# A weight decoder's rates per step changed, four steps without decoding, and two VectorE chains staggered

## The chip, the core and the metric

The kernel runs as one program on one core of a Trainium2 chip. The time is device microseconds (us) of that core for one execution; where several executions were timed, their median is given. Engines are named as in the profile: PE is TensorE (PEld its weight loads), DVE is VectorE, ACT is ScalarE, POOL is GpSimd, SP issues the DMAs.

## The reference: clustered attention and two MLPs

The inputs q, k, v are (2, 8, 768, 64) in single precision; the five weight matrices of the MLPs are in double precision, and the kernel reads each number as two 32-bit words. In short:

```
mask   = argmax(q_n @ c_n) == argmax(k_n @ c_n)      # cluster of each query and key
attn   = softmax(where(mask, q @ k^T / 8, -1e9))
x      = (attn @ v), heads side by side               # 1536 tokens x 512
x      = (sigmoid(x @ w_gate) * (x @ w_val)) @ w_out  # first MLP,  512 -> 1536 -> 512
out    = (relu(x @ w_in)^2) @ w_out2                  # second MLP, 512 -> 2048 -> 512
```

## The kernel before: steps, two instruction streams beside each other, and their order

**Precision.** Every matmul operand is a pair of fp32r tiles, a high part (rounded copy) and a low part (what is left). A product takes three matmuls of 128 columns of weights by 512 tokens: high by high, high by low, low by high (L339 to L341, and L416).

**Steps.** After the attention, which ends near 300 us, the two MLPs are a list of steps. The tokens are in three groups g = 0, 1, 2 of 512. The hidden layer is cut into slices j of 128, and four slices make a chunk (CH = 4). Per chunk there are 12 steps of the first layer (named "g" in the first MLP, gate and value of slice j for group g, 24 matmuls; named "i" in the second, 12 matmuls), and then 12 steps "o" of the output layer, in the order g outer, j inner, 12 matmuls each. An "o" step adds slice j into four PSUM banks, d = 0 to 3, one for each 128 of the 512 outputs. With the last j of a chunk the four sums are complete: DVE adds each into an SBUF tile `part` (L422; in the first chunk ACT copies it, L420). In the last chunk of the first MLP `part` is the second MLP's x: ACT makes its high part (`x_hi`, L427), DVE the low part (`x_lo`, L428), d after d. Below, o8 to o11 are the output weights of that chunk, i0 to i3 the first weights of the second MLP. The first steps of the second MLP run in the order (i0,g0), (i1,g0), (i0,g1), (i1,g1), (i0,g2), (i1,g2), and then i2 and i3.

**Decoding.** A weight slice comes from HBM as 512 KB of 64-bit numbers (`wraw`, two buffers) and is made into high and low parts by three stages, each a few instructions (`SLOTS`): stage 1 is `wmag` on ACT (L210) and L235, L239 on DVE; stage 2 is `wtop` (L242), `wmag` (L246) on DVE and the high part on ACT (L224); stage 3 is L215, L227, L230 on DVE, which ends with the low part. Stage 3's first instruction is followed by the fetch of the next raw slice into the buffer that it has read, on SP's queue.

**What sets the order.** The order is written out while the program is built. Each engine runs its own instructions in that order, and waits on the others by semaphores. Ahead of each step `decode(n)` adds `RATE` of the step's layer to a credit (at most 3.0) and places one decoding stage for each whole credit, provided that a buffer is free. Whatever is still missing for step n + 1 is placed at once. Then the step itself is placed, with its evictions. `presplit` makes the high and low parts of an "o" step's activations (`shi` on ACT, L382; `slo` on DVE, L383) four steps ahead; it has five buffers, so `shi` waits until PE has finished the "o" step that used its buffer, five "o" steps before. PSUM has four banks `bank_a` and four `bank_b`; "o" steps take `bank_b` for g = 0 and 2, `bank_a` for g = 1, the other steps `bank_a`. An "i" step's bank is emptied by ACT's relu (L375, written to `sg`) and its square (L376).

```
RATE = {"g": 2.25, "i": 1.25, "o": 1.25}
```

Of the kernel before, what the change touches and what calls it, by code (L numbers as in the profile page):

```python
# [14 lines left out]
ALU = mybir.AluOpType  # L15
# [56 lines left out]
def cluster_attention_two_mlps(  # L72
# [13 lines left out]
    nc = tc.nc  # L86
    B, H, S, D = q.shape
    NCL = centroids.shape[1]
    P = 128
# [3 lines left out]
    F1 = w_gate.shape[1]  # L93
# [6 lines left out]
    NG = B * S // TG  # L100

    def f32(ap):
        return ap.bitcast(F32)
# [5 lines left out]
    def x_tiles():  # L109
        return [[xp.tile([P, KD, TG], F32R, name=f"x_{t}{g}") for t in ("hi", "lo")] for g in range(NG)]  # L110
# [7 lines left out]
    CH = 4  # L118
    NA, NW, NWO = CH + 2, 4, CH + 2
    steps = []  # L120
# [17 lines left out]

    AHEAD = 4

    RATE = {"g": 2.25, "i": 1.25, "o": 1.25}
    pools = {}

    def open_weights():
# [122 lines left out]
    flight, credit = [], [0.0]  # L267
# [7 lines left out]
    def slot(n):  # L275

        moved = False
        for state in list(flight):
            d, parts, at = state
            if at == 1 and not buffer_free(d, n):  # L280
                break
            for x in SLOTS[at]:
                parts[x]()
            state[2] += 1
            moved = True
            if state[2] == len(SLOTS):
                flight.remove(state)
        if not moved and not flight and decoded[0] < len(weights):
            d = decoded[0]
            if buffer_free(d, n + 2):  # L290
                flight.append([d, decode_next(), 0])
                for x in SLOTS[0]:
                    flight[-1][1][x]()
                flight[-1][2] = 1
                moved = True
        return moved

    def decode(n):
        credit[0] = min(credit[0] + RATE[steps[n][1]], 3.0)
        while credit[0] >= 1.0 and slot(n):  # L300
            credit[0] -= 1.0

        while any(first_use[key] <= min(n + 1, len(steps) - 1) and key not in W for key in weights[: decoded[0] + 1]):
            need = [k for k in weights if first_use[k] <= n + 1 and k not in W]
            if not slot(n):
                assert all(first_use[k] > n for k in need), (n, need)
                break

    with tc.manual_schedule():
# [22 lines left out]
        def bank(side):  # L332
            return pools[side].tile([P, TG], F32, name=f"bank_{side}")
# [10 lines left out]
        act, parts, banks, split, sgs = {}, {}, {}, {}, {}  # L344
# [41 lines left out]
        def outer(step):  # L386
            mlp, _, j, g = step
            if step[0] == 2 and g == NG - 1 and j >= F2 // P - CH:

                if j == F2 // P - 1:  # L390
                    for d in range(KD):
                        for jj in range(F2 // P - CH, F2 // P):
                            outer_part((mlp, "o", jj, g), (d,))
                return
            outer_part(step, range(KD))

        def outer_part(step, ds_):
            mlp, _, j, g = step
            hi, lo = split[step]
            chunk = j // CH  # L400
            first, last = j % CH == 0, j % CH == CH - 1
            final = j == (F1 if mlp == 1 else F2) // P - 1
            w = W["o", mlp, j]
            for d in ds_:
                ds = slice(d * P, (d + 1) * P)
                if first:
                    banks[g, d] = bank("ba"[g % 2])
                bk = banks[g, d]

                pairs = (  # L410
                    [(w[:, 0, ds], hi), (w[:, 0, ds], lo), (w[:, 1, ds], hi)]
                    if mlp == 1
                    else [(hi[:, ds], w[:, 0]), (hi[:, ds], w[:, 1]), (lo[:, ds], w[:, 0])]
                )
                for n, (st, mv) in enumerate(pairs):
                    nc.tensor.matmul(bk, st, mv, start=(first and n == 0), stop=(last and n == 2))  # L416
                if last:
                    if chunk == 0:
                        parts[g, d] = pools["part"].tile([P, TG], F32, name=f"part{g}_{d}")
                        nc.scalar.copy(parts[g, d], bk)  # L420
                    else:
                        nc.vector.tensor_tensor(out=parts[g, d], in0=bk, in1=parts[g, d], op=ALU.add)  # L422
                    if final and mlp == 1:
                        if 2 not in xin:
                            xin[2] = x_tiles()
                        h, l = (t[:, d] for t in xin[2][g])
                        nc.scalar.copy(h, parts[g, d])  # L427
                        nc.vector.tensor_tensor(out=l, in0=parts[g, d], in1=f32(h), op=ALU.subtract)  # L428
                    elif final:
                        b, c = divmod(g * KD + d, NB)  # L430
                        nc.sync.dma_start(
                            out=out[b * S : (b + 1) * S].rearrange("(p c) d -> c p d", c=NB)[c], in_=parts[g, d]
                        )


        with ExitStack() as ac:
# [418 lines left out]
            for n in range(N + LAG + 4):  # L855
# [27 lines left out]
                if u is not None:  # L883
                    e = pp.tile([P, S], F32, name="p")
                    nc.scalar.activation(  # L885
                        out=e.rearrange("p (m n) -> p m n", m=2),
# [47 lines left out]
        with ExitStack() as mc:  # L934
            pools["o"] = mc.enter_context(tc.tile_pool(name="wop", bufs=NWO, reuse_waits="tile"))
            pools["part"] = mc.enter_context(tc.tile_pool(name="part", bufs=1, reuse_waits="tile"))
            pools["split"] = mc.enter_context(tc.tile_pool(name="split", bufs=AHEAD + 1, reuse_waits="tile"))
            pools["b"] = mc.enter_context(tc.tile_pool(name="ps_b", bufs=4, space=PSUM, reuse_waits="tile"))

            run = {"g": gated, "i": relu2, "o": outer}  # L940
            for n, step in enumerate(steps):
                if n < 2:
                    continue
                if n + AHEAD < len(steps) and steps[n + AHEAD][1] == "o":
                    presplit(steps[n + AHEAD])
                decode(n)
                run[step[1]](step)
# [29 lines left out]
```

## Time and profile before

| what | value |
|---|---|
| median of three runs | 862.56 us (861.41 to 864.62) |
| the profiled execution | 861.74 us, of which its span is 860.0 us |
| PE busy | 814.5 us, 95% of the span |
| DVE, ACT, POOL busy | 621.5, 448.7, 215.1 us |
| granted clock of PE, mean | 0.981 of full speed |
| slice 28 of 40 (580.5 to 602.0 us) | PE busy 5 tenths; every slice beside it 9 |
| a weight's DMA, issue to landing | 3.3 us (output weights), 3.6 to 3.8 us (the others) |

The page gives busy time by engine, then 40 slices of the span, then the chain of work that ended last, then groups of instructions. A row of a timeline has the start and the duration in us, engine, line, operation, output <- inputs, and in brackets how long the engine was idle before it and who released it. PE's matmuls are pipelined, so that the distance between two starts, not the duration, is what one costs. The same holds on DVE, where a following instruction starts before the recorded end of the one before.

### The profile page before, as it was taken

The page shows a single profiled execution, that of the slowest core. Times are in us where ns is not written, and L with a number is a line of the kernel's source. Part 1 is how long each engine was busy: PE and PEld are TensorE (multiplying, and loading weights), DVE is VectorE, ACT ScalarE, POOL GpSimd, SP SyncE. Part 2 cuts the span into 40 slices and gives each one's busy share as a digit, 9 for nine tenths or more (in the row PEclk, how much of TensorE's full clock was granted, in tenths as well). Part 3 has the DMA queues.
Part 4 walks back from the last instruction along what each step waited for, and adds up shares of the span by engine and source line. Part 5 has one row for each costly group of instructions (what it writes and reads, how often), then busy time and mean ns, then how long its engine had stood idle before and what let it go on. Part 6 is the DMA issues. An engine that isn't in the chain of part 4 may idle for free.

```text
span 860.0 us, 11716 instructions
## 1 busy us (share of the span) xinstructions
PE 814.5 (95%) x4069; PEld 694.7 (81%) x4069; DVE 621.5 (72%) x1129; ACT 448.7 (52%) x900; POOL 215.1 (25%) x339
## 2 busy tenths in 40 slices
PE   7697998998999999999999999995999999999998
PEld 5587888998999888788888888784888888888886
DVE  5596997898998557864678647887879589588033
ACT  7586797898888223441233123333755652552530
POOL 1467798898898200000000000000000000000000
PEclk9898999999999999999999999998999999999999
DMA  9764845855631212230222112211223123120012
GB/s 203 176 135 120 180 110 129 184 115 131 148 103 40 68 50 74 74 98 24 74 74 73 50 50 74 64 59 50 77 71 122 50 74 98 50 74 24 1 50 98
DMA packets 68107, 75.67 MB, mean 88 GB/s; under 512 B 29680, under 2 KB 56304, under 8 KB 68048
## 3 DMA queue, kind: packets, MB, share of 16 engines
q1 hardware_dynamic: 68048, 74.93, 32.7%
q8 instruction: 32, 0.52, 0.3%
q14 instruction: 27, 0.22, 0.1%
HBM read 45.12 MB, written 3.15 MB: 56 GB/s over the span
## 4 chain that ended last, share of the span: by engine, by line
PE 77%; DVE 9%; ACT 4%; DMA 3%; POOL 3%; issue 2%; SPq 1%; POOLq 0%; ACTq 0%; DVEq 0%
PE bank_b L416 15%; PE bank_a L340 12%; PE bank_a L339 12%; PE bank_a L341 12%; PE bank_a L416 8%; PE t L765 6%; PE s L747 6%; PE o L783 3%; PE o L784 3%; PE t L590 1%; DMA st_q<-lo_q 1%; DVE part L422 1%; DMA x<-oc 1%; DVE x_lo L428 1%; ACT x_hi L427 1%
## 5 line engine op out<-in xcount | busy, mean ns | idle before, releaser
L339 PE MATMUL bank_a<-x_hi,w 128*128 128x512 f32 x480 | 188.9, 394 | 8.8 <-ACT sg L375 8.8
L340 PE MATMUL bank_a<-x_lo,w 128*128 128x512 f32 x480 | 190.0, 396 | 0.5 <-POOL x_lo L813 0.5
L341 PE MATMUL bank_a<-x_hi,w 128*128 128x512 f32 x480 | 188.3, 392 | 0.0
L339 PEld LDWEIGHTS bank_a<-x_hi,w 128*128 128x128 f32 x480 | 90.6, 189 | 30.3 <-ACT sg L375 9.2
L773 DVE TENSOR_TENSOR pt_lo<-t,pt_hi 128x384 fp32r<-128x384 f32 x192 | 97.5, 548 | 23.8 <-ACT pt_hi L767 23.0
L383 DVE TENSOR_TENSOR slo<-act,shi 128x512 fp32r<-128x512 f32 x84 | 57.6, 687 | 71.4 <-ACT shi L382 67.4
L340 PEld LDWEIGHTS bank_a<-x_lo,w 128*128 128x128 f32 x480 | 90.6, 189 | 20.8 <-POOL x_lo L813 1.0
L341 PEld LDWEIGHTS bank_a<-x_hi,w 128*128 128x128 f32 x480 | 90.5, 189 | 20.4
L818 POOL TENSOR_SCALAR p<-p,nm,ones 128x768 f32<-128x768 f32 x96 | 95.7, 997 | 20.1 <-DVE nm L817 12.8
L765 PE MATMUL t<-ident,p 128*128 128x128 f32 x576 | 83.8, 282 | 16.1 <-POOL lo_q L546 14.0
L864 DVE TENSOR_REDUCE nm<-s 128x1 f32<-128x768 f32 x96 | 91.0, 948 | 4.5 <-PE s L747 4.4
L885 ACT ACTIVATE p<-s,nm 128x768 f32<-128x768 f32 x96 | 88.4, 921 | 7.5 <-DVE nm L817 3.8
L767 ACT CAST pt_hi<-t 128x384 fp32r<-128x384 f32 x192 | 83.6, 488 | 16.0 <-DMA x_lo<-pt_hi 7.8
L765 PEld LDWEIGHTS t<-ident,p 128*128 128x128 f32 x576 | 69.4, 145 | 23.1 <-POOL lo_q L546 15.0
L747 PE MATMUL s<-st_k,st_q 128*128 128x384 f32 (+1 forms) x336 | 81.4, 365 | 2.2 <-ACT p L885 1.1
L365 DVE TENSOR_TENSOR act<-bank_a,sg 128x512 f32<-128x512 f32 x36 | 24.9, 692 | 76.9 <-PE bank_a L341 73.0
L416 PE MATMUL bank_b<-wo,shi 128*128 128x512 f32 x256 | 79.0, 390 | 0.0
L224 ACT CAST w<-wtop 128x512 fp32r<-128x512 f32 x38 | 23.6, 621 | 99.5 <-DVE wtop L242 99.5
L382 ACT CAST shi<-act 128x512 fp32r<-128x512 f32 x84 | 51.1, 615 | 32.1 <-PE bank_b L416 20.0
L783 PE MATMUL o<-pt_hi,vt 128*128 128x384 f32 x192 | 66.2, 345 | 0.4 <-ACT oc L789 0.4
L784 PE MATMUL o<-pt_lo,vt 128*128 128x384 f32 x192 | 65.4, 341 | 0.0
L416 PE MATMUL bank_b<-shi,wo 128*128 128x512 f32 x192 | 60.7, 392 | 1.5 <-DVE wo L230 1.5
(136 smaller groups left out, 1401.6 us busy)
## 6 DMA issues: line engine op xcount, KB each, us to landing
wraw<-in_moe_w_out_dram SPq DMA_DIRECT2D x28, 512.0 KB, 3.3
wraw<-in_moe_w_in_dram SPq DMA_DIRECT2D x16, 512.0 KB, 3.8
x<-oc SPq DMA_DIRECT2D x64, 96.0 KB, 2.9
wraw<-in_moe_w_gate_dram SPq DMA_DIRECT2D x11, 512.0 KB, 3.6
wraw<-in_moe_w_val_dram SPq DMA_DIRECT2D x11, 512.0 KB, 3.7
st_k<-hi_k SPq DMA_DIRECT2D x26, 192.0 KB, 4.1
st_q<-hi_q SPq DMA_DIRECT2D x26, 192.0 KB, 4.0
nat_v<-in_v_dram SPq DMA_DIRECT2D x8, 384.0 KB, 3.2
```

What stands on the lines that cost most here:

```text
L339: nc.tensor.matmul(bk, w[:, 0, ks], mov_hi[:, kk], start=(kk == 0), stop=False)
L340: nc.tensor.matmul(bk, w[:, 0, ks], mov_lo[:, kk], start=False, stop=False)
L341: nc.tensor.matmul(bk, w[:, 1, ks], mov_hi[:, kk], start=False, stop=(kk == KD - 1))
L416: nc.tensor.matmul(bk, st, mv, start=(first and n == 0), stop=(last and n == 2))
L747: nc.tensor.matmul(st[:, m, :NH], Q[i, e][: DEPTH[a], a, c * P : (c + 1) * P], K[i, e][: DEPTH[a], a, m * NH : (m + 1) * NH], start=(a == ...
L765: nc.tensor.transpose(tp[:, m, :], Pt[u][:, c * P : (c + 1) * P], ident)
L773: nc.vector.tensor_tensor(out=lo, in0=tp, in1=f32(hi), op=ALU.subtract)
L783: nc.tensor.matmul(o, vt, hi[:, c, :], start=(c == 0), stop=False)
L784: nc.tensor.matmul(o, vt, lo[:, c, :], start=False, stop=(c == NB - 1))
L818: nc.gpsimd.tensor_scalar(out=p, in0=p, scalar1=nm[:, 3:4], scalar2=ones, op0=ALU.mult, op1=ALU.mult)
L864: nc.vector.tensor_reduce(out=nms[n][:, 0:1], in_=st[n][:, :, :NH], axis=AX.XY, op=ALU.max, negate=True)
L885: nc.scalar.activation(out=e.rearrange("p (m n) -> p m n", m=2), in_=st.pop(n)[:, :, :NH], func=AF.Exp, bias=nms[n][:, 0:1], accum_out=nms ...
```

## The change: what it does

Three edits. The decoding rates per step become 2.8, 1.4 and 0.85 for "g", "i" and "o". In the last four steps of the first MLP (j = 8 to 11 of group 2) the rate is 0, so no stage of a decode is placed there. And where x's low parts are made, `x_lo` of sum d is placed behind `part` of sum d + 1, and the last one behind all.

```
--- before.py
+++ after.py
@@ -138,7 +138,7 @@
 
     AHEAD = 4
 
-    RATE = {"g": 2.25, "i": 1.25, "o": 1.25}
+    RATE = {"g": 2.8, "i": 1.4, "o": 0.85}
     pools = {}
 
     def open_weights():
@@ -296,7 +296,10 @@
         return moved
 
     def decode(n):
-        credit[0] = min(credit[0] + RATE[steps[n][1]], 3.0)
+        mlp, layer, j, g = steps[n]
+
+        rate = 0.0 if (mlp, layer) == (1, "o") and j >= F1 // P - CH and g == NG - 1 else RATE[layer]
+        credit[0] = min(credit[0] + rate, 3.0)
         while credit[0] >= 1.0 and slot(n):
             credit[0] -= 1.0
 
@@ -401,6 +404,7 @@
             first, last = j % CH == 0, j % CH == CH - 1
             final = j == (F1 if mlp == 1 else F2) // P - 1
             w = W["o", mlp, j]
+            lows = []
             for d in ds_:
                 ds = slice(d * P, (d + 1) * P)
                 if first:
@@ -420,17 +424,24 @@
                         nc.scalar.copy(parts[g, d], bk)
                     else:
                         nc.vector.tensor_tensor(out=parts[g, d], in0=bk, in1=parts[g, d], op=ALU.add)
+                    if lows:
+                        low_part(*lows.pop(0))
                     if final and mlp == 1:
                         if 2 not in xin:
                             xin[2] = x_tiles()
                         h, l = (t[:, d] for t in xin[2][g])
                         nc.scalar.copy(h, parts[g, d])
-                        nc.vector.tensor_tensor(out=l, in0=parts[g, d], in1=f32(h), op=ALU.subtract)
+                        lows.append((l, parts[g, d], f32(h)))
                     elif final:
                         b, c = divmod(g * KD + d, NB)
                         nc.sync.dma_start(
                             out=out[b * S : (b + 1) * S].rearrange("(p c) d -> c p d", c=NB)[c], in_=parts[g, d]
                         )
+            for low in lows:
+                low_part(*low)
+
+        def low_part(lo, whole, hi):
+            nc.vector.tensor_tensor(out=lo, in0=whole, in1=hi, op=ALU.subtract)
 
 
         with ExitStack() as ac:
```

**DVE, end of the first MLP.** In these rows `w_4137` and `w_4184` are the tiles of i2 and i3, `w1_68` that of i1, and `part2_d`, `x_lo2` belong to token group 2. Before:

```order
L215 SCALAR_TENSOR_TENSOR wbody_6334<-wraw_6264,wmag_6335 128x512
L227 TENSOR_TENSOR wtop_6336<-wtop_6336,w_4137 128x512
L230 TENSOR_TENSOR w_4137<-wtop_6336,wbody_6334 128x512
L235 TENSOR_SCALAR wbody_6400<-wraw_6314 128x512
L239 SCALAR_TENSOR_TENSOR wbody_6400<-wraw_6314,wbody_6400 128x512
L242 SCALAR_TENSOR_TENSOR wtop_6402<-wmag_6401,wbody_6400 128x512
L246 TENSOR_SCALAR wmag_6401<-wtop_6402 128x512
L215 SCALAR_TENSOR_TENSOR wbody_6400<-wraw_6314,wmag_6401 128x512
L227 TENSOR_TENSOR wtop_6402<-wtop_6402,w_4184 128x512
L230 TENSOR_TENSOR w_4184<-wtop_6402,wbody_6400 128x512
L422 TENSOR_TENSOR part2_0_4918<-bank_b_6367,part2_0_4918 128x512
L428 TENSOR_TENSOR x_lo2_6238<-part2_0_4918,x_hi2_6237 128x512
```

After:

```order
L444 TENSOR_TENSOR x_lo1_6236<-part1_3_4842,x_hi1_6235 128x512
L426 TENSOR_TENSOR part2_0_4904<-bank_b_6353,part2_0_4904 128x512
L426 TENSOR_TENSOR part2_1_4909<-bank_b_6357,part2_1_4909 128x512
L444 TENSOR_TENSOR x_lo2_6238<-part2_0_4904,x_hi2_6237 128x512
L426 TENSOR_TENSOR part2_2_4914<-bank_b_6361,part2_2_4914 128x512
L444 TENSOR_TENSOR x_lo2_6238<-part2_1_4909,x_hi2_6237 128x512
L426 TENSOR_TENSOR part2_3_4919<-bank_b_6365,part2_3_4919 128x512
L444 TENSOR_TENSOR x_lo2_6238<-part2_2_4914,x_hi2_6237 128x512
L444 TENSOR_TENSOR x_lo2_6238<-part2_3_4919,x_hi2_6237 128x512
L215 SCALAR_TENSOR_TENSOR wbody_6304<-wraw_6184,wmag_6305 128x512
L227 TENSOR_TENSOR wtop_6306<-wtop_6306,w1_68 128x512
L230 TENSOR_TENSOR w1_68<-wtop_6306,wbody_6304 128x512
```

The decodes of i2 and i3 stood ahead of group 2's sums, and now stand behind them; so does the last stage of i1, which stood ahead of group 1's sums before. `x_lo` of sum d is one place behind `part` of sum d + 1.

**ACT, the same place.** `x_hi1`, `x_hi2` are the high parts of groups 1 and 2, and `sg` the first relu of the second MLP, which empties the bank of (i0,g0). Before:

```order
L427 CAST x_hi1_6235<-part1_3_4850 128x512
L224 CAST w_4137<-wtop_6336 128x512
L210 ACTIVATE wmag_6401<-wraw_6314 128x512
L224 CAST w_4184<-wtop_6402 128x512
L427 CAST x_hi2_6237<-part2_0_4918 128x512
L427 CAST x_hi2_6237<-part2_1_4923 128x512
L427 CAST x_hi2_6237<-part2_2_4928 128x512
L427 CAST x_hi2_6237<-part2_3_4933 128x512
L210 ACTIVATE wmag_6451<-wraw_6384 128x512
L375 ACTIVATE sg_6470<-bank_a_6456 128x512
```

After:

```order
L433 CAST x_hi1_6235<-part1_3_4842 128x512
L433 CAST x_hi2_6237<-part2_0_4904 128x512
L433 CAST x_hi2_6237<-part2_1_4909 128x512
L433 CAST x_hi2_6237<-part2_2_4914 128x512
L433 CAST x_hi2_6237<-part2_3_4919 128x512
L210 ACTIVATE wmag_6423<-wraw_6264 128x512
L378 ACTIVATE sg_6442<-bank_a_6428 128x512
```

Two high parts of weights and a `wmag` have left the place between groups 1 and 2.

**DVE, first "o" steps of the first chunk.** `wo_4704` before and `wo_4688` after are the tile of the fourth output weight o3 (`wbody`, `wtop`, `wmag` with the numbers just below it belong to its decode); the `slo` are the presplits of the steps placed there. Before:

```order
L383 TENSOR_TENSOR slo_4678<-act_4216,shi_4677 128x512
L235 TENSOR_SCALAR wbody_4681<-wraw_4609 128x512
L239 SCALAR_TENSOR_TENSOR wbody_4681<-wraw_4609,wbody_4681 128x512
L383 TENSOR_TENSOR slo_4700<-act_4429,shi_4699 128x512
L242 SCALAR_TENSOR_TENSOR wtop_4683<-wmag_4682,wbody_4681 128x512
L246 TENSOR_SCALAR wmag_4682<-wtop_4683 128x512
L215 SCALAR_TENSOR_TENSOR wbody_4681<-wraw_4609,wmag_4682 128x512
L227 TENSOR_TENSOR wtop_4683<-wtop_4683,wo_4704 128x512
L230 TENSOR_TENSOR wo_4704<-wtop_4683,wbody_4681 128x512
```

After:

```order
L386 TENSOR_TENSOR slo_4658<-act_4165,shi_4657 128x512
L235 TENSOR_SCALAR wbody_4661<-wraw_4576 128x512
L239 SCALAR_TENSOR_TENSOR wbody_4661<-wraw_4576,wbody_4661 128x512
L386 TENSOR_TENSOR slo_4684<-act_4216,shi_4683 128x512
L242 SCALAR_TENSOR_TENSOR wtop_4663<-wmag_4662,wbody_4661 128x512
L246 TENSOR_SCALAR wmag_4662<-wtop_4663 128x512
L386 TENSOR_TENSOR slo_4704<-act_4434,shi_4703 128x512
L215 SCALAR_TENSOR_TENSOR wbody_4661<-wraw_4576,wmag_4662 128x512
L227 TENSOR_TENSOR wtop_4663<-wtop_4663,wo_4688 128x512
L230 TENSOR_TENSOR wo_4688<-wtop_4663,wbody_4661 128x512
```

Stage 2 of o3 stood behind the third `slo` of this stretch's presplits together with stage 3, and is now one step earlier, so that only stage 3 stands behind that `slo`. In the two later chunks of the first MLP the fourth output weight ends a step earlier in the same way.

## Rows read from the trace of the kernel before

**Rows 1.** Waits of TensorE (PE) from 300 us on: us in total, times, longest.

```profile
PE bank_a L339 <- ACT sg L375: 8.8, 1, 8.8
PE bank_b L416 <- DVE wo L230: 1.5, 3, 1.1
```

**Rows 2.** Timeline of PE, 583 to 614 us: start, duration, line, operands, idle before.

```profile
592.57 0.39 PE L341 MATMUL bank_a<-x_hi,w 128*128 128x512 f32 x1
601.74 0.80 PE L339 MATMUL bank_a<-x_hi,w 128*128 128x512 f32 x1 [8.78 <-ACT sg L375]
...
606.01 0.39 PE L340 MATMUL bank_a<-x_lo,w 128*128 128x512 f32 x1
```

**Rows 3.** Window: busy PE, PEld, DVE, ACT, POOL; granted clock; DMA share, GB/s.

```profile
596.00:598.00 2.00, 0.00 (x0) 0.00 (x0) 1.32 (x3) 0.62 (x1) 0.00 (x0) 0.50 0.00 0
```

**Rows 4.** Timeline of ScalarE (ACT), 575 to 614 us.

```profile
580.59 0.62 ACT L427 CAST x_hi<-part 128x512 fp32r<-128x512 f32 x1 [1.36 <-DVE part L422]
...
601.10 0.58 ACT L375 ACTIVATE sg<-bank_a 128x512 f32<-128x512 f32 x1
```

**Rows 5.** Timeline of VectorE (DVE), 575 to 612 us.

```profile
577.83 0.68 DVE L422 TENSOR_TENSOR part<-bank_a,part 128x512 f32<-128x512 f32 x1
...
579.87 0.68 DVE L422 TENSOR_TENSOR part<-bank_a,part 128x512 f32<-128x512 f32 x1
581.24 0.69 DVE L428 TENSOR_TENSOR x_lo<-part,x_hi 128x512 fp32r<-128x512 f32 x1 [0.69 <-ACT x_hi L427]
...
585.81 0.69 DVE L242 SCALAR_TENSOR_TENSOR wtop<-wmag,wbody 128x512 f32<-128x512 f32 x1
...
586.99 0.69 DVE L215 SCALAR_TENSOR_TENSOR wbody<-wraw,wmag 128x512 f32<-128x512 uint32 x1
587.60 0.69 DVE L227 TENSOR_TENSOR wtop<-wtop,w 128x512 f32<-128x512 f32 x1
588.32 0.69 DVE L230 TENSOR_TENSOR w<-wtop,wbody 128x512 fp32r<-128x512 f32 x1
...
593.31 0.68 DVE L422 TENSOR_TENSOR part<-bank_b,part 128x512 f32<-128x512 f32 x1
...
600.66 0.69 DVE L428 TENSOR_TENSOR x_lo<-part,x_hi 128x512 fp32r<-128x512 f32 x1 [0.68 <-ACT x_hi L427]
```

**Rows 6.** Timeline of PE, 578.5 to 583 us.

```profile
579.65 0.62 PE L416 MATMUL bank_b<-shi,wo 128*128 128x512 f32 x2
...
581.69 0.39 PE L416 MATMUL bank_b<-shi,wo 128*128 128x512 f32 x1
581.91 0.39 PE L339 MATMUL bank_a<-x_hi,w 128*128 128x512 f32 x1
```

**Rows 7.** Timeline of PE, 355.2 to 360.5 us.

```profile
356.57 0.86 PE L416 MATMUL bank_b<-shi,wo 128*128 128x512 f32 x2
...
358.80 0.73 PE L416 MATMUL bank_b<-shi,wo 128*128 128x512 f32 x2 [1.13 <-DVE wo L230]
...
360.30 0.39 PE L416 MATMUL bank_b<-shi,wo 128*128 128x512 f32 x1
```

**Rows 8.** Timeline of DVE, 346 to 361 us.

```profile
358.05 0.69 DVE L230 TENSOR_TENSOR wo<-wtop,wbody 128x512 fp32r<-128x512 f32 x1
```

**Rows 9.** Timeline of PE, 100 to 300 us: rows with an idle time.

```profile
108.51 0.92 PE L765 MATMUL t<-ident,p 128*128 128x128 f32 x6 [2.59 <-POOL lo_q L546]
...
140.35 0.92 PE L765 MATMUL t<-ident,p 128*128 128x128 f32 x6 [2.44 <-POOL lo_q L546]
...
173.16 0.92 PE L765 MATMUL t<-ident,p 128*128 128x128 f32 x6 [2.19 <-POOL lo_q L546]
```

**Rows 10.** Windows behind these three idle times, columns as in Rows 3.

```profile
108.50:116.00 7.50, 7.49 (x52) 7.28 (x52) 7.45 (x17) 7.31 (x19) 6.99 (x10) 1.00 0.11 27
...
140.40:146.00 5.60, 5.60 (x29) 5.42 (x30) 4.78 (x11) 4.66 (x12) 4.33 (x7) 0.70 0.11 27
...
173.20:178.00 4.80, 4.80 (x35) 4.63 (x35) 4.80 (x11) 4.80 (x13) 4.46 (x7) 1.00 0.10 23
```

More of the change, by code (lines that the diff above doesn't have):

```diff
@@ L139, in cluster_attention_two_mlps @@
     AHEAD = 4
-    RATE = {"g": 2.25, "i": 1.25, "o": 1.25}
+    RATE = {"g": 2.8, "i": 1.4, "o": 0.85}
     pools = {}
@@ L298, in decode @@
     def decode(n):
-        credit[0] = min(credit[0] + RATE[steps[n][1]], 3.0)
+        mlp, layer, j, g = steps[n]
+        rate = 0.0 if (mlp, layer) == (1, "o") and j >= F1 // P - CH and g == NG - 1 else RATE[layer]
+        credit[0] = min(credit[0] + rate, 3.0)
         while credit[0] >= 1.0 and slot(n):
@@ L403, in outer_part @@
             w = W["o", mlp, j]
+            lows = []
             for d in ds_:
@@ L422, in outer_part @@
                         nc.vector.tensor_tensor(out=parts[g, d], in0=bk, in1=parts[g, d], op=ALU.add)
+                    if lows:
+                        low_part(*lows.pop(0))
                     if final and mlp == 1:
@@ L427, in outer_part @@
                         nc.scalar.copy(h, parts[g, d])
-                        nc.vector.tensor_tensor(out=l, in0=parts[g, d], in1=f32(h), op=ALU.subtract)
+                        lows.append((l, parts[g, d], f32(h)))
                     elif final:
@@ L433, in outer_part, with low_part @@
                         )
+            for low in lows:
+                low_part(*low)
+        def low_part(lo, whole, hi):
+            nc.vector.tensor_tensor(out=lo, in0=whole, in1=hi, op=ALU.subtract)
         with ExitStack() as ac:
```

## The prediction

> **What bounds the kernel now.** I read the page's slices first (the table above has the one that matters): in nearly every slice of the MLPs TensorE is busy for nine tenths or more, and one stands out with five. So the MLPs take as long as TensorE's matmuls, plus what TensorE waits. The view of its waits from 300 us on names all of them [rows 1]: one of 8.8 us for an ACT relu, and three of together 1.5 us, the longest 1.1, for the low part of an output weight. A change to decoding and evictions can only give back these, and what hangs on them, or add new ones.
>
> The long wait lies at the passage to the second MLP. The last matmul before it starts at 592.57, the next at 601.74 [rows 2]. Undisturbed matmuls start 0.227 us apart, nine in 579.65 to 581.69 [rows 6]. So 9.17 - 0.23 = 8.94 us are lost there. While TensorE idles its granted clock falls to half, 0.50 in 596 to 598 [rows 3], and it is slow after the wait too: the ten distances from 601.74 to 606.01 take 4.27 us instead of 2.27, a loss of 2.0 [rows 2]. The passage costs 10.9 us.
>
> What ended the wait is read on the two engines behind it. ACT's relu at 601.10 [rows 4] empties the bank that (i0,g2) needs, and stands in ACT's order behind the four x_hi of group 2; each of those needs its `part`. VectorE begins group 2's sums only at 593.31 [rows 5], although TensorE finished them at 581.69 + 0.39 = 582.1 [rows 6]. Up to then VectorE was in a chain for group 1 (577.83 to 585.81) and two weight decodes (585.81 to 593.31) [rows 5]. The chain is slow: `part` at 579.87, x_hi on ACT at 580.59, x_lo at 581.24 [rows 4, 5]; with 0.61 for x_lo the next link starts 1.98 us later, and VectorE has idled 0.69 of it. Four links are 7.98 us (577.83 to 585.81).
>
> **The change part by part.**
>
> *Staggering.* Let the first `part` start at 0. x_hi starts 0.72 later and x_lo 1.37 later, as before, but the second `part` runs in between. From then on VectorE has something ready: at its pitch of 0.61 (586.99 to 587.60 [rows 5]) the order part, part, x_lo, part, x_lo, part, x_lo, x_lo gives the third x_lo at 3.81. The fourth `part` starts at 3.20, so its x_hi at 3.92 and its x_lo at 4.57; VectorE is free at 5.18. The chain costs 5.18 instead of 7.98.
>
> A rule of the Trainium skill speaks against this edit: the page VectorE: DVE Perf Modes, section The DRAIN you can't avoid, says that the next instruction does not start before the pipe has emptied, that semaphores between instructions cost nothing extra, and that only their number counts. By that, reordering the same eight instructions gives nothing, and the chain stays at 7.98. The rows differ: an instruction of 0.69 us is followed 0.61 later by the next [rows 5], and 0.69 of each link is marked as idle until ACT's x_hi, which is the time that the new order fills.
>
> *No decoding in the last four steps.* Between the chains of groups 0 and 1 VectorE had 16 instructions and has 11 (counted in the two orders), five less at some 0.6: 3.0 us. With 2.8 from group 0's stagger, group 1's chain starts near 577.83 - 5.8 = 572.0 and ends near 577.2. Nothing stands between it and group 2's any more, so group 2's chain starts when TensorE ends the first sum: 579.65 + 0.39 = 580.04 [rows 6]. Its x_lo is done near 585.2. TensorE wants it for (i0,g2), four steps of 12 x 0.227 = 2.72 after 581.91, at 592.8. The 8.94 us and the half clock go. What is late next is on ACT nothing: its relu of (i0,g0) now stands behind x_hi's end and one `wmag`, some 584 to 585, seven us before its bank is wanted.
>
> *The price: i1.* Its last stage now stands behind group 2's chain: L215 at 585.2, L227 0.61 later, L230 0.72 later (586.99, 587.60, 588.32 [rows 5]), at 586.55, done 0.69 later at 587.24. The first matmul to read this low part is the third of (i1,g0), 14 x 0.227 after 581.91: 585.08. TensorE waits 587.24 - 585.08 = 2.2 us. Behind that matmul everything else on TensorE waits with it. Bounds: if VectorE were held only by TensorE's last sum (582.08, then 1.37, 0.61, 0.61, 0.72, 0.69), 1.0; if the stagger gave nothing, 2.2 + 2.8 = 5.0. I take 2.2, from the rows' own pitches.
>
> Does a wait of 2.2 lower the clock? Three waits of that size stand in the attention: 2.59, 2.44 and 2.19 us [rows 9]. Behind the first and the third the granted clock is 1.00, behind the second 0.70 over 5.6 us [rows 10]. One in three; at half clock for 0.6 of 5.6 = 3.4 us the loss is 1.7 us, near the 2.0 of the passage. I take no fall as the likelier case.
>
> *The rates.* With 2.8 per "g" step the fourth output weight of each chunk of the first MLP ends earlier. For o3 stage 2 moves one step forward; L242 and L246 (585.81 to 586.99: 1.18 us [rows 5]) no longer stand ahead of its last stage. That ended at 358.05 + 0.69 = 358.74 [rows 8] and will end near 357.56. The nine distances from 356.57 to 360.30 took 3.73 instead of 2.04: 1.7 us lost, and the wait itself was 1.13 [rows 7], so the matmul was due between 357.25 (without the stretched one before) and 357.67. Some 0.3 remain: 1.4 won. The other two waits are 1.5 - 1.1 = 0.4 together [rows 1]; their weights now end a whole step (2.72) earlier, so they go. As at o3, more is lost than waited (1.7 for 1.1); I take 0.4 each instead of 0.2, so 0.8, and 0.4 to 1.4 as bounds.
>
> *Moved at no cost.* In the second MLP all decodes come later. TensorE waits for none of them before [rows 1], since the weights are ready 6 to 22 steps ahead (counted in the order). After the change it is 2 to 6 steps for the first chunk's output weights and 4 to 14 later, 2.72 us a step. That margin is the cover; where it is gone, a weight costs what o3 cost, 1.7. The fetches move with stage 3, in the same sequence on SP's queue; i3's is now issued behind group 2's chain, near 586, and i3 is first used nine steps after (i0,g0). The rate of 0.85 still gives 12 x 1.4 + 12 x 0.85 = 27.0 stages a chunk, where 8 weights of 3 stages need 24.
>
> *Sum.* 10.9 - 2.2 + 1.4 + 0.8 = 11.0 us (10.94 and 2.16 unrounded). The profiled execution took 861.74, so 850.7; it is 0.8 below the median of the three runs, 862.56. Against that median I predict 851.5.
>
> **The rivals.**
>
> A: the wait for i1 takes the clock with it. For it: a wait of 2.44 did so, and 8.8 did. Against: two of three did not. 851.5 + 2.0 = 853.5.
>
> B: the stagger gives nothing, because VectorE or ACT hold each other at each link anyway; then group 2's chain ends 2.8 us later, the wait for i1 is 5.0 and the clock falls: 851.5 + 2.8 + 2.0 = 856.3. For it: the links of before never show two of these instructions closer. Against: the idle time in each link is put down to ACT alone. The rule of the page above leads here.
>
> C: the wait for i1 is covered. With the lower bound of 1.0 and a sum won in full: 850.0. It needs VectorE to be early at every link.
>
> D: no gain: what was idle at the passage returns elsewhere, for instance as ACT in-order behind the high part of i2, which needs VectorE after i1. Then (i1,g1)'s relu is late and the banks close again. For it: ACT's order has that copy between the first two relus. Against: i2's stage 2 is the third instruction behind i1's end, some 2 us, while the bank in question is wanted two steps later. It would have to cost 8.94 again: near 861.
>
> E: slower. The second MLP's weights run out: at 0.85 a step, output weights come one step late and each costs up to 1.7 with the clock up; it needs seven such waits (7 x 1.7 = 11.9) to be slower than before, 863.5. It decides from the point at which a weight's last stage stands in the same step as its use; the order has two steps at least. Against it, that margin; for it, that VectorE may be late itself by more than a step after the passage.
>
> **How the numbers follow.** Forecast (850.5 to 852.8) 0.55; A 0.2; B 0.1; C 0.06; D 0.05; E 0.04. A measurement of this kernel can tell about 0.5%, 4.3 us, from no change. Forecast, A, B and C are faster by more (856.3 is 6.3 below 862.56): 0.91. D is within: 0.05. E at 863.5 and beyond: 0.04 for slower. The range goes from C's 850.0, less 1 for the spread of runs (the three of before lie 1.2 below to 2.1 above their median), so 849.0, to 856.0, just short of B, and leaves out some 0.18.
>
> **What would show it.** In the waits of TensorE after the change the row for an ACT relu is gone, and one wait for a VectorE low part (L230) of 1.0 to 3 us stands at 584 to 587, once; no other MLP wait above 0.5. The granted clock stays at 1.00 through the passage (in A it falls to 0.5 for some us). VectorE's chain for a group takes some 5.2 us, and group 2's starts near 580 rather than 593. The span ends near 849. The prediction is wrong in its core if the chain still takes 8 us, if TensorE waits at (i0,g2) again, or if waits for weights appear behind 620 us.

## The result and the profile after

Changed kernel: median 852.57 us (851.15 to 852.97, four runs); kernel before in the same series: 863.59 (861.41 to 864.76). The ratio is 0.987, 95% interval 0.985 to 0.990. A second series of the same two kernels gave medians of 852.06 and 861.58, a ratio of 0.989 (0.986 to 0.991). The prediction was 851.5 in a range of 849.0 to 856.0. The profiled execution took 852.56 us, with a span of 850.8 and a mean granted clock of 0.986.

The waits of TensorE from 300 us on, answering to [rows 1]:

```profile
PE bank_a L344 <- DVE w L230: 2.1, 1, 2.1
PE bank_b L420 <- DVE wo L230: 0.7, 2, 0.5
```

The wait for an ACT relu is gone. One wait of 2.1 us for the low part of i1 has come, and two for output weights are left. TensorE at the passage, answering to [rows 2, 6] (start, duration, idle before in brackets):

```profile
578.80 0.39 PE L342 MATMUL bank_a<-x_hi,w 128*128 128x512 f32 x1
...
581.75 0.39 PE L343 MATMUL bank_a<-x_lo,w 128*128 128x512 f32 x1
584.25 0.50 PE L344 MATMUL bank_a<-x_hi,w 128*128 128x512 f32 x1 [2.12 <-DVE w L230]
584.59 0.39 PE L342 MATMUL bank_a<-x_hi,w 128*128 128x512 f32 x1
...
585.51 0.58 PE L343 MATMUL bank_a<-x_lo,w 128*128 128x512 f32 x1
585.89 0.63 PE L344 MATMUL bank_a<-x_hi,w 128*128 128x512 f32 x1
586.31 0.63 PE L342 MATMUL bank_a<-x_hi,w 128*128 128x512 f32 x1
```

The wait stands where it was predicted, at the third matmul of (i1,g0). TensorE then runs at its usual pitch for a while (four distances of 0.23 from 584.59 to 585.51), and only then slows: the next are 0.38 and 0.42. VectorE beside it, answering to [rows 5]:

```profile
576.96 1.37 DVE L426 TENSOR_TENSOR part<-bank_b,part 128x512 f32<-128x512 f32 x2 [3.13 <-PE bank_b L420]
578.39 0.69 DVE L444 TENSOR_TENSOR x_lo<-part,x_hi 128x512 fp32r<-128x512 f32 x1
579.00 0.68 DVE L426 TENSOR_TENSOR part<-bank_b,part 128x512 f32<-128x512 f32 x1
579.60 0.68 DVE L444 TENSOR_TENSOR x_lo<-part,x_hi 128x512 fp32r<-128x512 f32 x1
580.20 0.68 DVE L426 TENSOR_TENSOR part<-bank_b,part 128x512 f32<-128x512 f32 x1
580.80 1.46 DVE L444 TENSOR_TENSOR x_lo<-part,x_hi 128x512 fp32r<-128x512 f32 x2
582.18 0.68 DVE L215 SCALAR_TENSOR_TENSOR wbody<-wraw,wmag 128x512 f32<-128x512 uint32 x1
...
583.50 0.69 DVE L230 TENSOR_TENSOR w<-wtop,wbody 128x512 fp32r<-128x512 f32 x1
```

The chain of eight takes 582.18 - 576.96 = 5.22 us and has no idle time inside. Its start waits for TensorE (3.13 us idle), and i1's last stage stands right behind it, ended by 583.50 + 0.69 = 584.19. ScalarE, answering to [rows 4]:

```profile
580.92 0.62 ACT L433 CAST x_hi<-part 128x512 fp32r<-128x512 f32 x1 [0.57 <-DVE part L426]
...
582.01 0.58 ACT L378 ACTIVATE sg<-bank_a 128x512 f32<-128x512 f32 x1
```

The relu that was the last to come now runs 0.3 us after its sum is there. And the fourth output weight of the first chunk (o3), VectorE's last stage and then TensorE, answering to [rows 7, 8]:

```profile
355.93 0.69 DVE L230 TENSOR_TENSOR wo<-wtop,wbody 128x512 fp32r<-128x512 f32 x1
```

```profile
356.68 0.72 PE L420 MATMUL bank_b<-shi,wo 128*128 128x512 f32 x2 [0.20 <-DVE wo L230]
```

Its wait was 1.13 and is 0.20. The wait of 0.54 is new, in the second MLP, at the fourth output weight of its first chunk (called o23 in the expectations below). VectorE, ScalarE, then TensorE:

```profile
616.33 0.69 DVE L386 TENSOR_TENSOR slo<-act,shi 128x512 fp32r<-128x512 f32 x1 [1.90 <-ACT shi L385]
...
620.53 0.68 DVE L242 SCALAR_TENSOR_TENSOR wtop<-wmag,wbody 128x512 f32<-128x512 f32 x1
621.25 0.43 DVE L246 TENSOR_SCALAR wmag<-wtop 128x512 int32<-128x512 int32 x1
622.43 0.69 DVE L386 TENSOR_TENSOR slo<-act,shi 128x512 fp32r<-128x512 f32 x1 [0.75 <-ACT shi L385]
623.04 0.68 DVE L215 SCALAR_TENSOR_TENSOR wbody<-wraw,wmag 128x512 f32<-128x512 uint32 x1
...
624.36 0.69 DVE L230 TENSOR_TENSOR wo<-wtop,wbody 128x512 fp32r<-128x512 f32 x1
```

```profile
621.25 0.62 ACT L224 CAST wo<-wtop 128x512 fp32r<-128x512 f32 x1 [2.72 <-DVE wtop L242]
621.78 1.14 ACT L385 CAST shi<-act 128x512 fp32r<-128x512 f32 x2
```

```profile
618.51 0.39 PE L420 MATMUL bank_b<-wo,slo 128*128 128x512 f32 x1
618.74 0.62 PE L420 MATMUL bank_b<-wo,shi 128*128 128x512 f32 x2
...
624.18 0.39 PE L420 MATMUL bank_b<-wo,shi 128*128 128x512 f32 x1
625.10 0.50 PE L420 MATMUL bank_b<-wo,shi 128*128 128x512 f32 x1 [0.54 <-DVE wo L230]
```

The stage is not late because VectorE had too much to do: VectorE stands idle for 0.75 us in front of it, at the `slo` of the sixth output step. The buffer for that step's `shi` is the one of the first output step, five before, and was free long since: TensorE ended that step at 618.51 + 0.39 = 618.90. But in ScalarE's order this `shi` stands right behind the high part of o23 itself (L224), and there ScalarE idles 2.72 us until VectorE has made o23's `wtop` (L242). The 1.90 us in front of 616.33 end with a `shi` too, which stands behind the high part of the weight before and a relu. So VectorE and ScalarE wait for each other in turn, and VectorE falls behind TensorE: o23's last stage is placed ahead of the second output step, which began at 618.74, and it starts at 623.04.

**Where the time went, by stretches.** A stretch is counted on TensorE from the first matmul of one kind of step to the first of the next kind. "Passage" is the stretch from the first matmul of (i0,g0) to the first output matmul of the second MLP. The later stretches of the same form, where nothing waits, take 33.13 us, and output stretches of one group 10.88 to 10.92.

| stretch, us | before | after | won |
|---|---|---|---|
| first output matmul of all | starts at 348.60 | starts at 347.67 | 0.93 |
| group 0's output stretch, chunks 1, 2, 3 of the first MLP | 12.61, 11.40, 11.42 | 11.42, 10.92, 10.92 | 2.17 |
| passage | 44.11 | 37.18 | 6.93 |
| group 0's output stretch, first chunk of the second MLP | 10.92 | 11.77 | -0.85 |
| first output matmul to the last matmul | 507.29 | 499.04 | 8.25 |

With the first row that is 9.18 us, the difference of the two profiled executions. The first row is no work of the change. Up to 315 us (times of the kernel before) all the kernels of this document run the same instructions in the same order on every engine, and from there to the first output matmul, 144 matmuls, TensorE takes 33.17 us in each of the twelve profiles.

### The profile page after: what moved, and what is told of

It reads as the page before. It is cut to its first block, busy times and chain, and to the rows that moved or that the text cites. A ratio compares the mean times of both kernels' runs of the same rounds, so it can differ in the third digit from the quotient of the medians.

```text
span 850.8 us, 11707 instructions
## 1 busy us (share of the span) xinstructions
PE 815.1 (96%) x4069; PEld 695.2 (82%) x4069; DVE 622.0 (73%) x1129; ACT 449.5 (53%) x900; POOL 214.6 (25%) x339
## 4 chain that ended last, share of the span: by engine, by line
PE 83%; DVE 5%; ACT 4%; POOL 2%; DMA 2%; issue 2%; SPq 1%; POOLq 0%; ACTq 0%; DVEq 0%
PE bank_b L420 16%; PE bank_a L343 12%; PE bank_a L344 12%; PE bank_a L342 12%; PE bank_a L420 9%; PE s L758 6%; PE t L776 6%; PE o L794 3%; PE o L795 3%; PE t L601 1%; DMA st_q<-lo_q 1%; DVE pt_lo L784 1%; POOL p L829 1%; PE t L548 1%; DMA x_lo<-pt_hi 1%
## 5 line engine op out<-in xcount | busy, mean ns | idle before, releaser
L224 ACT CAST w<-wtop 128x512 fp32r<-128x512 f32 x38 | 23.7, 623 | 103.1 <-DVE wtop L242 103.1
L242 DVE SCALAR_TENSOR_TENSOR wtop<-wmag,wbody 128x512 f32<-128x512 f32 x66 | 45.3, 687 | 23.8 <-ACT wmag L210 21.8
```

## The experiments

The table has every run; the start of the first output matmul moved between 342.97 and 348.60, by 2.4 us between four executions of one kernel, so the last column tells the kernels apart better than a single time does.

| kernel | ratio to before (95%) | passage | group 0's output stretches, first MLP | first of the second MLP | first output matmul to last matmul |
|---|---|---|---|---|---|
| before | 1 | 44.11 | 12.61, 11.40, 11.42 | 10.92 | 507.29 |
| after, four profiles | 0.987 and 0.989 | 37.18; 35.58, 35.54, 35.54 | 11.4, 10.9, 10.9 | 11.75 to 11.78 | 499.04; 497.47, 497.35, 497.37 |
| stagger alone | 0.9875 (0.985 to 0.990) | 33.99 | 12.60, 11.41, 11.41 | 10.92 | 497.15 |
| rates and stop, no stagger | 0.996 (0.994 to 0.998) | 43.28 | 11.43, 10.92, 10.92 | 11.78 | 505.16 |
| stop alone | 0.991 (0.989 to 0.993) | 37.58 | 12.61, 11.43, 11.43 | 10.91 | 500.79 |
| stop and stagger, old rates | 0.986 (0.9835 to 0.988) | 33.13 | 12.59, 11.40, 11.41 | 10.92 | 496.28 |
| rates and stagger, no stop | 0.984 (0.982 to 0.9865) | 33.13 | 11.45, 10.92, 10.91 | 10.92 | 494.16 |
| after, i1 finished first | 0.984 (0.981 to 0.987) | 33.12 | 11.41, 10.92, 10.92 | 10.92 | 494.12 |
| the same, rate of "i" 1.6 | 0.984 (0.981 to 0.987) | 33.13 | 11.41, 10.92, 10.92 | 10.92 | 494.12 |

**Stagger alone.** Against the changed kernel:

```
-    RATE = {"g": 2.8, "i": 1.4, "o": 0.85}
+    RATE = {"g": 2.25, "i": 1.25, "o": 1.25}
...
-        rate = 0.0 if (mlp, layer) == (1, "o") and j >= F1 // P - CH and g == NG - 1 else RATE[layer]
+        rate = RATE[layer]
```

> The kernel before with the stagger alone (old rates, decoding in the last four steps as before). Theory of the chain (mine): each of the three chains takes 5.2 instead of 8.0 us, so group 2's chain starts 2 x 2.8 = 5.6 us earlier, near 587.7 instead of 593.3, the relu of (i0,g0) ends near 593.4, TensorE waits for it 0.5 to 1 us instead of 8.8 and the clock stays up: 10 us less than before, ratio 0.988; the three waits for output weights (1.5 us) stay. Theory of the decodes (rival): what stood between the chains made TensorE wait, and the order within a chain is worth nothing (also what the Trainium skill's page VectorE: DVE Perf Modes says in The DRAIN you can't avoid): ratio 1.000, wait still above 7 us.

Waits of TensorE from 300 us on, and VectorE at group 2's chain:

```profile
PE bank_b L420 <- DVE wo L230: 1.5, 3, 1.1
PE bank_a L342 <- ACT sg L378: 0.5, 1, 0.5
```

```profile
584.28 0.69 DVE L230 TENSOR_TENSOR w<-wtop,wbody 128x512 fp32r<-128x512 f32 x1
584.89 1.28 DVE L426 TENSOR_TENSOR part<-bank_b,part 128x512 f32<-128x512 f32 x2
...
588.73 1.46 DVE L444 TENSOR_TENSOR x_lo<-part,x_hi 128x512 fp32r<-128x512 f32 x2
590.11 0.42 DVE L235 TENSOR_SCALAR wbody<-wraw 128x512 int32<-128x512 int32 x1
```

The output weights wait as before, and decodes still stand in front of group 2's chain, but the chain takes 590.11 - 584.89 = 5.22 us; the wait for the relu shrinks from 8.8 to 0.5. This edit alone wins 10.1 us of the passage and the same time as the whole change.

**Rates and stop, no stagger.** Against the changed kernel:

```
-                    if lows:
-                        low_part(*lows.pop(0))
...
-                        lows.append((l, parts[g, d], f32(h)))
+                        low_part(l, parts[g, d], f32(h))
```

> The changed kernel without the stagger (new rates, no decoding in the last four steps). Theory of the chain: group 1's chain from about 574.8 to 582.8, group 2's to 590.8 in before's times, then i1's last stage, done near 592.8, wanted at 585.1: one wait of 6.5 to 8 us for a VectorE low part at (i1,g0), clock at half behind it, 9.5 us lost of the 10.9; the output weights still save 2.2 and one later wait costs 0.8: ratio 0.995 to 0.999. Theory of the decodes: as the changed kernel, ratio 0.987.

Waits, VectorE in group 2's chain, and a window during TensorE's wait:

```profile
PE bank_a L344 <- DVE w L230: 7.2, 1, 7.2
PE bank_b L420 <- DVE wo L230: 0.7, 2, 0.5
```

```profile
579.05 0.68 DVE L426 TENSOR_TENSOR part<-bank_b,part 128x512 f32<-128x512 f32 x1
580.42 0.69 DVE L442 TENSOR_TENSOR x_lo<-part,x_hi 128x512 fp32r<-128x512 f32 x1 [0.68 <-ACT x_hi L431]
581.03 0.68 DVE L426 TENSOR_TENSOR part<-bank_b,part 128x512 f32<-128x512 f32 x1
```

```profile
582.00:584.00 2.00, 0.00 (x0) 0.00 (x0) 1.60 (x3) 1.97 (x4) 0.00 (x0) 0.50 0.00 0
```

Without the stagger a link takes 581.03 - 579.05 = 1.98 us again, with 0.68 idle. With the two chains of group 1 and group 2 one behind the other, i1's last stage comes 7.2 us late: the long wait has changed its name and place, and hardly its size.

**i1 finished first.** Against the changed kernel:

```
-        rate = 0.0 if (mlp, layer) == (1, "o") and j >= F1 // P - CH and g == NG - 1 else RATE[layer]
+        rate = 0.0 if (mlp, layer) == (1, "o") and j >= F1 // P - CH and g == NG - 1 and ("i", 1) in W else RATE[layer]
```

> The changed kernel, but decoding stops only once i1 is decoded: its last stage now stands between the chains of groups 1 and 2 on VectorE, where the changed kernel's VectorE idles 3.1 us; 2.0 us of work fit there. My theory: the wait of 2.1 us at (i1,g0) goes and with it the half clock behind it (1.8 us), and the wait for the fourth output weight of the second MLP's first chunk (0.8 us lost) shrinks since all later stages come a step earlier: 848 to 849, ratio to before 0.982 to 0.983, granted clock 1.00 throughout the passage. Rival: group 2's chain is pushed back and the wait only moves to (i0,g2), or the clock falls there without a wait: 851 to 853, as the changed kernel.

All waits of TensorE from 300 us on:

```profile
PE bank_b L420 <- DVE wo L230: 0.2, 1, 0.2
```

VectorE uses what the changed kernel leaves idle in front of group 2's chain (3.13 us there) for i1's last stage. The wait, what hung on it and the late o23 go together, and the passage is at its undisturbed 33.12.

**The same, rate of "i" 1.6.**

```
-    RATE = {"g": 2.8, "i": 1.4, "o": 0.85}
+    RATE = {"g": 2.8, "i": 1.6, "o": 0.85}
```

> As e3_i1_first, and the rate of the second MLP's first layer 1.6 instead of 1.4: the fourth output weight of its first chunk is finished five steps ahead of its use instead of three (two in the changed kernel). If the wait of 0.5 us at that weight comes from the lower rates, it is gone here in any case: 847.5 to 848.5 and no wait of TensorE in the second MLP. Rival: more stages per step delay the relus on ACT, and TensorE waits for banks: 849 or more.

Nothing changes: 494.12 both times. The weights of the second MLP came in time once i1 was not held back: the low part of o23 is ready 0.3 us ahead of its first use with the rate 1.4, and 6.6 us ahead with 1.6.

**The changed kernel again.** No edit, three more profiles. (The first expectation names a wrong start of the passage; its 33.1 us count from the first matmul of (i0,g0), as above.)

> The changed kernel once more, unedited, beside the other three. It asks two things: whether its ratio to the kernel before, 0.987, holds beside theirs on one chip, and whether the 2.1 us wait for the low part of i1 lowers the clock again. Theory (the clock falls after this wait as a rule): passage to the second MLP (first matmul of the last output stretch of the first MLP to the first output matmul of the second, 33.12 us where nothing waits) near 37.2 us as in the first profile, granted clock 0.50 for two microseconds behind the wait. Rival (it falls only now and then, as behind one of three such waits in the attention): passage near 35.3 (33.1 + 2.1), clock 1.00.

> The changed kernel, unedited, for its profile alone: does the 2.1 us wait for i1 lower the granted clock in this execution? In the first profile it did (passage 37.2 us), in the second not (35.6 us). Theory (it falls in some executions and not in others, the instructions being the same): passage either near 37.2 or near 35.6, nothing between; the wait itself 2.1 us again and the first output stretch of the second MLP 11.8 us again. Rival (the wait itself differs between executions): a wait other than 2.1 and a passage to match.

> As the look before it: passage near 37.2 with the clock at 0.50 behind the wait, or near 35.6 with the clock at 1.00; wait 2.1 us, first output stretch of the second MLP 11.8 us.

Windows behind the wait (busy time of PE, PEld, DVE, ACT, POOL; granted clock; DMA). First profile, then the second:

```profile
586.00:588.00 2.00, 2.00 (x6) 1.56 (x5) 1.90 (x5) 0.79 (x2) 0.00 (x0) 0.50 0.10 30
```

```profile
584.00:586.00 2.00, 2.00 (x11) 1.64 (x10) 1.93 (x4) 1.59 (x3) 0.00 (x0) 1.00 0.16 23
```

All four have a wait of 2.12 us at the same matmul. Behind it the clock fell in the first execution alone (six matmuls in two microseconds instead of eleven, which is 1.2 GHz instead of 2.4); the passage is 37.18 there and 35.54 to 35.58 in the others. The fall costs 1.6 us when it comes, in one of four.

**Stop alone.** Against the changed kernel:

```
-    RATE = {"g": 2.8, "i": 1.4, "o": 0.85}
+    RATE = {"g": 2.25, "i": 1.25, "o": 1.25}
...
-                    if lows:
-                        low_part(*lows.pop(0))
...
-                        lows.append((l, parts[g, d], f32(h)))
+                        low_part(l, parts[g, d], f32(h))
```

> Only the four steps without decoding: old rates 2.25, 1.25, 1.25, low parts right behind their own sum as before. In the order of VectorE nothing stands any more between the chains of groups 1 and 2 (12 instructions before), and i1 is finished ahead of group 1's chain. Theory: group 2's chain starts at the end of group 1's, 585.8 instead of 593.3 in the times of the kernel before, so the relu that TensorE waits for comes 7.5 us earlier; TensorE waits 8.9 - 7.5 = 1.4 us, passage 34.5, or 36.5 if that wait lowers the clock; output weights of the first MLP as before (12.6, 11.4, 11.4 us), first output stretch of the second MLP 11.8 as after (a late weight, 0.85 more). First output matmul to last: 507.3 - 9.6 + 0.85 = 498.6 (500.6 with the clock), ratio near 0.990. So either edit would win the passage alone, and the poor result of the stop with the new rates came from i1. Rival (the stop does nothing without the stagger, as in the run with new rates and stop): passage near 43, ratio 0.996 or above.

ScalarE and TensorE where the wait ends:

```profile
593.92 0.62 ACT L224 CAST w<-wtop 128x512 fp32r<-128x512 f32 x1 [1.36 <-DVE wtop L242]
594.45 0.59 ACT L378 ACTIVATE sg<-bank_a 128x512 f32<-128x512 f32 x1
```

```profile
595.09 0.80 PE L342 MATMUL bank_a<-x_hi,w 128*128 128x512 f32 x1 [2.72 <-ACT sg L378]
595.68 0.63 PE L343 MATMUL bank_a<-x_lo,w 128*128 128x512 f32 x1
596.11 0.63 PE L344 MATMUL bank_a<-x_hi,w 128*128 128x512 f32 x1
```

The mechanism was as expected, the size was not: 2.7 us of wait instead of 1.4, at half clock behind it. The relu stands behind a weight's high part on ScalarE, which VectorE only feeds after both chains. And o23 is not late here, against the expectation. So the stop alone does win most of the passage (6.5 of 10.9 us); it is the rates that take it away in the run without the stagger.

**Rates and stagger, no stop.** Against the changed kernel:

```
-        rate = 0.0 if (mlp, layer) == (1, "o") and j >= F1 // P - CH and g == NG - 1 else RATE[layer]
+        rate = RATE[layer]
```

> New rates and the stagger, decoding goes on in the last four steps. Theory (with the stagger the stop isn't needed, and all it does is to keep i1 back and o23 late): i1 is ready five steps ahead, ten decoding instructions (6.1 us) stand between the chains of groups 1 and 2, group 2's chain starts near 583 and its relu is done near 589, ahead of 592.8. No wait of TensorE above 0.3 at the passage, 33.1 us; output stretches of the first MLP 11.4, 10.9, 10.9, first of the second 10.9. First output matmul to last 494.1, as with i1 finished first; ratio near 0.984. Rival (the stop is a part of the gain): TensorE waits for the relu of (i0,g0) or for a weight as before, passage 36 or more, ratio 0.988 or above.

VectorE in front of group 2's chain:

```profile
577.71 0.69 DVE L230 TENSOR_TENSOR w<-wtop,wbody 128x512 fp32r<-128x512 f32 x1
578.32 1.28 DVE L426 TENSOR_TENSOR part<-bank_b,part 128x512 f32<-128x512 f32 x2
```

As the theory said, in every stretch. Decodes run right up to the chain, without an idle time in front of it, and the chain is still early enough. Against the stagger alone, the new rates win 2.1 us at the output weights of the first MLP and the last 0.9 of the passage (33.99 to 33.13). In the changed kernel the stop takes 494.16 to 497.4, so it costs 3.2 us, or 4.9 with the clock.

**Stop and stagger, old rates.** Against the changed kernel:

```
-    RATE = {"g": 2.8, "i": 1.4, "o": 0.85}
+    RATE = {"g": 2.25, "i": 1.25, "o": 1.25}
```

> The stop and the stagger with the old rates 2.25, 1.25, 1.25. It asks which edit delays i1 and o23. Theory (i1 is late only through the rates, o23 only through the stop): i1 is ready seven steps ahead, so the passage is 33.1 us at a clock of 1.00; the output stretches of the first MLP are as before, 12.6, 11.4, 11.4; the first output stretch of the second MLP is 11.8, since the weight o23 is ready two steps ahead only. First output matmul to last: 494.1 + 2.2 + 0.85 = 497.1; ratio near 0.988. Rival (the rate of 0.85 makes o23 late): that stretch is 10.9 and the whole 496.3. Rival (the stop delays i1 by itself): a wait for a VectorE low part of about 2 us at the third matmul of (i1,g0), passage 35 to 37, whole 499 or more.

Waits from 300 us on, and VectorE at o23:

```profile
PE bank_b L420 <- DVE wo L230: 1.5, 3, 1.1
```

```profile
618.87 0.69 DVE L386 TENSOR_TENSOR slo<-act,shi 128x512 fp32r<-128x512 f32 x1 [0.75 <-ACT shi L385]
...
620.80 0.69 DVE L230 TENSOR_TENSOR wo<-wtop,wbody 128x512 fp32r<-128x512 f32 x1
```

The passage is undisturbed, so i1 is late only with both the stop and the new rates. o23 was expected to be late here and is not: the first rival was right with its 496.3. Its last stage stands behind the same idle `slo` as in the changed kernel, with the same 0.75 us, but VectorE gets there 4.78 us after the first output matmul of the second MLP and not 6.45: the last stage of the weight before it has been placed ahead of the fourth output step's `slo` and not behind it. The low part is ready 1.0 us ahead of its use here, as with the stop alone, and 8.2 us ahead with rates and stagger but no stop. So the stop takes most of the cover and the new rates the rest; neither makes o23 late by itself, together they do.

## Why the prediction was right, and where its terms were off

*What bounds the kernel: right.* The 8.8 us wait and the half clock behind it went, and what the edits gave back was only what TensorE had waited, and what hung on these waits. Each of the three kernels that leave the rates as they were (stagger, stop, both) shortens the passage, by 6.5 to 11.0 us.

*The stagger: right.* Predicted 7.98 to 5.18 us a chain, measured 5.22; the run without it has 1.98 a link again. Rival B fell with it. The Trainium skill (VectorE: DVE Perf Modes, section The DRAIN you can't avoid) states that the next instruction does not start before the pipe has emptied and that semaphores between instructions cost nothing extra. It adds that a next instruction which is not held starts earlier. The rows fit that addition: instructions that are ready follow each other every 0.60 us in the new chain and 0.61 before, at a recorded 0.68 to 0.69. The section does not say that the order within a chain is worth nothing; the prediction and the expectation of the stagger alone concluded that from it. The conclusion left out the time in which VectorE stands still for ScalarE, and here that was a third of the chain.

*No decoding in the last steps: the step was right, its weight was not.* Group 2's chain did become bound by TensorE (3.13 us idle). But the forecast counted both edits towards the same 8.9 us, without asking whether one would do. With the stagger at the old rates the stop still wins 0.87 us (497.15 to 496.28); at the new rates it is worth nothing, and only its price remains.

*The price of i1: right.* Predicted 2.2 us at the third matmul of (i1,g0), measured 2.12 in all four profiles; with the slower first matmuls behind it the passage is 35.55 - 33.13 = 2.4 us over its undisturbed length. Predicted passage: 44.11 - 10.94 + 2.16 = 35.3.

*The clock: the likelier case was rightly chosen, and the first profile shows the other one.* Rival A had 0.2 and came in one of four. In the profiled execution it cost 37.18 - 35.55 = 1.6 us, where rival A had 2.0.

*The rates: right in sum.* 1.2 at o3 instead of 1.4, since 0.20 us of wait stretches the matmuls around it to 0.5; 0.48 and 0.50 at the two others, 0.98 instead of 0.8. Together 2.17 in the profiled execution, where 2.2 was predicted.

*Moved at no cost: wrong by 0.85 us.* This is the step that failed. The order had shown o23 two steps ahead of its use, and the prediction took 2.72 us for each step as cover. Places in an order are no times: VectorE began this last stage 4.3 us after TensorE began the step that it is placed in front of, after 1.90 and 0.75 us in which it stood idle for ScalarE. With stop and stagger at the old rates the stage has the same place in the order and began 2.6 us after that step, which the cover still bore. Due 0.23 us after 624.18, the low part was there at 624.36 + 0.69 = 625.05. That is what rival E named, VectorE late by more than a step, at one weight instead of seven and at 0.85 us instead of 1.7. The prediction had named two signs against itself that this wait meets: another wait in the MLPs above 0.5 (it is 0.54), and, as a sign that the core is wrong, a wait for a weight behind 620 us (it stands at 625.10). It shows the cover wrong, and not the chain or the passage, which came out as forecast.

The sum by these terms is 8.55 + 2.17 - 0.85 = 9.9 us in the three executions without a fall of the clock (497.4 against 507.29) and 8.25 in the first, where 11.0 was predicted. The steps that missed are o23 (0.85), i1's stretched matmuls (0.2) and, in the first profile, the clock (1.6). There 11.0 - 8.25 = 2.75 us are missing; 0.93 were won ahead of the first output matmul, which no term had and no edit made, and so the profiled 852.56 lies 1.9 above the 850.7 that the sum gave for it. That the medians of the first series differ by 863.59 - 852.57 = 11.0, the very sum of the prediction, is luck: the second series has 861.58 - 852.06 = 9.5, and the stretches give 8.25 to 9.9.

*Chance, and what stays open.* The first output matmul starts at 345.70 to 348.60 in the four profiles with the old rates and at 342.97 to 347.67 in the eight with the new; the changed kernel alone covers 345.29 to 347.67. The rates have no part in it: in every profile the last 33.17 us ahead of that matmul are the same, and ahead of these all engines run the same instructions in the same order, so only executions differ. Why they do stays open. And what decides whether the clock falls behind the same wait wasn't tried.

The best kernels are the changed one with i1 finished first and the one with rates and stagger but without the stop (494.1 us each from the first output matmul to the last, both at a ratio of 0.984).

## What to carry to other kernels

When two edits are aimed at one wait, price each with the other already in place: here either one was worth 6 to 10 us of the passage alone, and with the stagger in place the stop added 0.9 at the old rates and cost 3.2 or more at the new. In an in-order engine, look at idle times inside a chain of dependent instructions before thinning the work around it; putting the next link's independent instruction in between cost nothing here. A margin counted in steps of the consumer holds only while the engine that fills it keeps up with these steps: read its timeline for when it gets there, and for engines that wait for each other in turn.

## What the runs showed of the hardware

The granted clock does not answer to the length of a wait alone. After the same 2.12 us wait, in the same program, it fell to 0.50 once and stayed at 1.00 three times, and where it fell it did so more than a microsecond after TensorE had resumed (at 584.25; the starts up to 585.51 are at full speed). A wait of 2.72 (stop alone) ended at half clock, which is 0.50 in the window 596 to 598 behind it; one of 0.5 (stagger alone) left the passage 0.86 longer than undisturbed, as did 0.54 at o23 (0.85). The clock was 1.00 at both. So these short waits cost some 0.3 us more than the trace lists for them, in matmuls that start late or last longer beside them.
